# State attention and a gated causal convolution on one core: one PSUM pool of eight banks for three, and a new table of issue

## The chip, the core and the metric

The kernel runs on one core of a Trainium2 chip. Its engines run side by side, each through its own list of instructions in order: PE (TensorE: matmuls and transposes; PEld is its weight load), DVE (VectorE), ACT (ScalarE), POOL (GpSimd), and SP (SyncE), which here does nothing but issue the DMAs. An instruction waits for the data that it reads and for the buffer that it writes. PE writes to PSUM, a memory of eight banks of 128 partitions x 512 fp32 words; ACT and DVE read it there. All other tiles lie in SBUF.

The metric is the time of one execution in microseconds (us), as the median of several runs. One execution was recorded by the profiler; its rows are what this document reads.

## The reference

All inputs are fp32: `x` (8 batches, 8 heads, 512 rows, 64), `state` (8, 8, 32, 64), and three weights: two of 512 x 512 and a convolution of 5 taps x 512 channels (their values come as 64-bit floats and are decoded on the chip).

```python
scale = 1 / sqrt(D)
a     = softmax(scale * x @ state.T)          # (B,H,512,32)
xread = a @ state                             # (B,H,512,64)
a2    = softmax(scale * state @ x.T)          # (B,H,32,512)
sread = a2 @ x                                # (B,H,32,64)
u = concat([xread, sread], axis=2)            # heads side by side: (B,544,512)
gate_pre = sum over k in 0..4 of conv_w[k] * u shifted down by 4-k rows
y = (sigmoid(gate_pre) * (u @ w_val)) @ w_out # (B,544,512)
```

## The kernel before

**Tiles and steps.** Channels lie on the partitions: 512 channels are four blocks of 128, which are four pairs of heads. The program builds a list `steps` of small closures (one transpose, one softmax part, one tap, one projection tile) and then issues them in the order of a table of numbers, `ORDER` (L31 and on; the loop at L706 does it). A letter behind a number chooses the engine of a step that several can do: `a` ACT, `v` DVE, `g` POOL. Nothing else sets the order: each engine executes its instructions as the table lists them. The waits between engines come from the tiles. A tile name that has n buffers gives its n+1st tile the buffer of the first, and that tile's writer waits until all readers of the old one are done.

**The start.** SP loads the weights, the state and the first batch. `warm_up` (L243) multiplies the identity with itself, two matmuls to a step, four rows in the trace; nothing reads its result. The weights are decoded from their 64-bit words with elementwise steps: `words_scale`, `words_low` (L216), `words_clamp` (L221), `words_join` (L226) and `words_sign` (L231); those of `w_out` are then split into a high and a low part, `woh` and `wol`. `group_T` (L276, tile `sgp`) transposes the state of four batches.

**One batch.** Four `x_T` transposes (L309, `xTp`), copied to `xT`; the scores of state against x (L315; L337 for batches 0 to 2, tile `sc`), which serve both softmaxes. For the 512-row side: a transpose on DVE (L388, `sl`), the maximum `max_n` (L394), `sub_n` (L175, `sl<-sl,mx`), the exponential `exp_n` on ACT, the sums `sum_n` (L404 to L406), `scale_n` (L175, `ex<-ex,rc`), and `probs` (L412), a DVE transpose back. `high` and `low` split the result in two parts, `ah` and `al` (`combine` at L175 is the line of every two-operand elementwise step). For the 32-row side: `max_s` (L345), `exp_s`, transposes `exp_T` (L355, `e2p`), `state_read` (L365, `srp`), which also gives the tail its rows. `state_val` (L287, `sgv`) multiplies the state with `w_val`, and is split into `swh` and `swl`.

Then `read` (L421) writes the four tiles `xr` to PSUM. Per block of channels the convolution runs over `xr`: `gate_first` on ACT (L456), three `gate_tap` on DVE (L461), and the last tap as two steps, `gate_last` (L170 on ACT, L172 on DVE) and `gate_add` (L175, `acc<-acc,last`); `gate` on ACT makes the sigmoid by a tanh. Batch 0 is an exception: `read_conv` (L436) folds the taps into the matmul. `values` (L484) is six matmuls of 512 columns, `gated` (L487, `g`) multiplies gate and values, and `gh` (L162, L164, L166) and `gl` (L175) split the product for `project` (L492 to L494): twelve matmuls of 512 columns into one bank, then a copy to `o` and a store.

**The tail.** The 32 state rows of all batches go last, together: `tail_taps` (L518, `tacc`), `tail_values` (L544, `tval`), `tail_gated` (L548, `tg`) and two `tail_project` (`top`). Some projections of the last two batches stand between them.

**PSUM.** Three pools hold the eight banks: `tp` has two (`xTp`, `e2p`, `srp`, `srT`, `cwp`, `halo`), `sc` four (`sgp`, `sgv`, `sc`, `xr`) and `mm` two (`cwbp`, `warm`, `val`, `op`, `tval`, `top`). A tile takes the next bank of its own pool in turn.

Of the kernel before, what the change touches and what calls it, by code (L numbers as in the profile page):

```python
# [30 lines left out]
ORDER = """  # L31
41 50 5 8 0 53 10 107 42v 29 23 43 12 2 44v 11v 6 35 45 18 47 1 30v 13v 32v 14 105 15 915 916 917 918 114 59 3 36v 46
37 38v 919 920 921 922 16 17 19 31 48 104 39 52a 115v 40 60a 25 24v 110 108 106 83 33 61a 56 187 111a 55a 109a 21 51a
185 112 113a 54a 116 188 49a 186 26v 34 27 28 85 120 22v 58a 84v 86g 117 57a 62 288 193 66a 287 20a 118 189 194a 121
190a 195 122 124 285 87 125v 67a 89 103 123 191 196a 192a 64a 88 63a 119 126 65 133 77 134a 201 203 127 204 286 139 91
131 197 140a 198 202 132a 128g 130 295 142g 296a 289 141a 135 582 199 290a 90a 92g 216 136 129 217a 293 200 78a 71 205
79 294a 206v 386 93 207 291 143 80v 156 94 292a 101a 81 150 153 99a 144 137 208 184 72a 73 388 297 82 157 301 138a 385
147 298 158a 222 302 148 223a 303 102g 304 209g 74g 299 300 387 224 145 146a 213 225a 159g 168 210 226 164 227 75 97a
211a 169 165 149a 243v 228 212g 230 166a 242 76 214 314 315a 160 268 170a 244 487 215a 229a 245 167g 151 152a 395 389
235 171g 396a 161 486 390a 246 483 95a 231 264 218 247g 237 248 393 232 98g 249 394a 421 162a 219 238 422a 265 239 391  # L40
256 233g 100v 384 316 236v 392a 234 284 317a 423 251 266a 163g 257 220 305 96g 250a 267g 258a 397 318 252 424a 425 253
178 306g 322 313 485 254g 179v 307 319 399 255 308 269 175 398 484 401 402 309g 260 270g 176a 172 403 400 221a 323v
240g 68 325a 241 310 324 413 326 494 259g 271g 311a 173v 312g 327 261 329a 328 586 181 404 330 495a 492 342 262a 356
177 331 332 263v 343a 344 333v 182a 414a 69 272 493a 345 335 405g 337 334 350a 415 357 346 273a 338 180 488 406 364
347g 70a 348 339 407 358a 278 489v 183 365 412 349 336a 360 351 366a 408g 279a 584 340g 368 341 520 352 353 523a 280
274 367v 361 409 281 521a 410a 416a 359g 522 524 362g 282v 354g 426 355 369 434 436 275 441 428a 4 685 427 276a 411g
443 490 437 438 429 363g 430 583 370g 320 435a 491a 174 459 439g 371g 440 431 444 460 445 442a 321v 585 461g 455 683
496 500 497 277 501 378 432g 593 503 448 446g 682 433 589 456 379a 590a 380 375 504v 154 505 462g 463 498 499 155a 447
619 594v 417 587 506 376a 450 588a 464 467 465a 451 452 449v 507g 591 418 622v 502 453g 684 620a 419 420a 457a 454 372
508 621 509a 623 525 458g 511 373v 547 468 381 526 9 533 512 466g 527a 592a 549 550 783 510g 514 551 548a 781 552g  # L50
515a 382a 528 529 530 513a 566 535 553 692 531g 536 469v 782 595 534a 470g 516 599 885g 532 377 541v 567 784 517 597
554 596 686 555 602 537 474 600 693a 283 540 690 687a 598 688 480 383 603g 691a 556a 689a 604 542 543 538g 475v 539
601 780 694 879a 481a 605 482 568g 791 7 699 544 695 613 558 476 696 792a 606g 700 614a 562 787 698 607 697 624 569g
610 559 788a 632 701 789 790a 634 545g 710 640a 560g 557g 546 477 702g 563 639 608a 646 785 609g 641 471 478a 786a
564a 711a 642 635 681 479 643 661 633v 636 648 649 644g 611 561g 518 793 565g 472a 645 662 374 663a 612a 637g 650 647v
794 657 625 473 703 651v 795 797 519a 664g 638 881a 658 615 627 579 796 580a 712 626a 704 652 718 719a 713a 616 798
705g 581 628 720 886g 570 721v 799 629 630g 573 659a 706 722 631 707v 571a 800 723 731 653 574a 617 708g 745 738 665
811 733 734 732a 654 660g 746a 735 576 801g 666 747 655a 736v 737 667a 748 749 740 577a 656g 668g 802 756 739a 757
750v 817 725a 803 804g 724 678 818a 741 726 820a 882g 727 679a 758a 675 669 821 728 751 575 812a 676a 742 578 618a 709
714 805 806a 743g 819 822 729v 730 670a 744 715 809 883g 760 810a 845v 813 807g 831v 752 759g 830 761 671 832 833 753  # L60
762a 763v 834 764 765 672 835g 572 844 846 716 766a 808 847 823 855 848 836 673a 767g 754v 755v 856 837 863 814 815
849g 825 850 826 717v 864 816a 777 677 774 880v 838a 900 887a 884g 778a 865a 779 839 840 841 857a 674 842v 775v 771
902 888v 768 858v 772a 824a 843 899 859 866v 827 901 769a 828g 904 903 860 889 851 829 861a 891 862g 852 853a 905 773
894 854v 680 906 890 892 870 776 893 871a 895 907g 896 873 872 874a 908v 897v 867 898g 912 868a 913a 909 770 869 914
875 910v 911 876 877a 878
""".split()


# [666 lines left out]
```

## Time and profile before

| what | value |
| --- | --- |
| median of 3 runs | 247.87 us (246.74 to 247.98) |
| the profiled execution | 247.3 us, of which the span 245.5 us |
| busy | PE 231.2 us, DVE 206.3, ACT 151.0, POOL 127.0 |
| share of PE in the chain that ended last | 62% |
| moved by DMA | 22.88 MB |

The span runs from the first instruction to the last on the chip; the profiled execution has 1.8 us beside it. In the rows below, L with a number is a line of the kernel, `out<-in` names the tiles, `xN` counts instructions, and what stands in square brackets at the end of a row of the timeline is the idle time ahead of it and the instruction that ended this idle time. In rows of groups, the busy time in us and the mean of one in ns stand behind the first bar, the idle time behind the second. In rows of windows come, after the stretch and its length, the busy time of PE, PEld, DVE, ACT and POOL, the granted clock of PE, the DMA share and GB/s.

### The profile page before, as it was taken

The page shows a single profiled execution, that of the slowest core. Times are in us where ns is not written, and L with a number is a line of the kernel's source. Part 1 is how long each engine was busy: PE and PEld are TensorE (multiplying, and loading weights), DVE is VectorE, ACT ScalarE, POOL GpSimd, SP SyncE. Part 2 cuts the span into 40 slices and gives each one's busy share as a digit, 9 for nine tenths or more (in the row PEclk, how much of TensorE's full clock was granted, in tenths as well). Part 3 has the DMA queues.
Part 4 walks back from the last instruction along what each step waited for, and adds up shares of the span by engine and source line. Part 5 has one row for each costly group of instructions (what it writes and reads, how often), then busy time and mean ns, then how long its engine had stood idle before and what let it go on. Part 6 is the DMA issues. An engine that isn't in the chain of part 4 may idle for free.

```text
span 245.5 us, 5051 instructions
## 1 busy us (share of the span) xinstructions
PE 231.2 (94%) x1955; PEld 167.7 (68%) x1955; DVE 206.3 (84%) x325; ACT 151.0 (62%) x321; POOL 127.0 (52%) x101
## 2 busy tenths in 40 slices
PE   7976999899999999999999999999999999978994
PEld 7953463366677884866787778666766768867882
DVE  3299999999898998899899898998997899987200
ACT  2056977788647875754787769785696475433110
POOL 3001146289959267793575689928758380131200
PEclk9999999999999999999999999999999999999999
DMA  6939987000320309213801021110110302300224
GB/s 194 312 105 341 340 190 169 7 3 0 88 78 10 85 24 277 62 28 88 225 34 53 3 96 62 69 43 3 43 44 3 132 0 85 128 0 3 85 76 138
DMA packets 34549, 22.88 MB, mean 93 GB/s; under 512 B 26058, under 2 KB 29150, under 8 KB 34526
## 3 DMA queue, kind: packets, MB, share of 16 engines
q1 hardware_dynamic: 34526, 22.57, 30.2%
q8 instruction: 15, 0.25, 0.4%
q14 instruction: 8, 0.07, 0.1%
HBM read 13.65 MB, written 8.91 MB: 92 GB/s over the span
## 4 chain that ended last, share of the span: by engine, by line
PE 62%; DVE 24%; DMA 5%; issue 4%; ACT 2%; SPq 1%; DVEq 0%; ACTq 0%
PE val L484 12%; PE op L492 11%; PE op L494 10%; PE op L493 10%; DMA vw<-w_val 4%; PE xTp L309 3%; DVE acc L461 3%; PE xr L421 3%; DVE tacc L518 3%; PE srp L365 3%; DVE g L487 2%; PE e2p L355 2%; PE sgv L287 2%; PE sc L315 2%; DMA ow<-w_out 2%
## 5 line engine op out<-in xcount | busy, mean ns | idle before, releaser
L461 DVE SCALAR_TENSOR_TENSOR acc<-xr,cw,acc 128x509 f32<-128x509 f32 (+2 forms) x84 | 60.6, 739 | 3.8 <-ACT xt L457 2.7
L492 PE MATMUL op<-woh,gh 128*128 128x512 f32 x128 | 52.1, 407 | 1.5 <-DVE g L487 1.1
L494 PE MATMUL op<-woh,gl 128*128 128x512 f32 x128 | 50.4, 394 | 0.0
L493 PE MATMUL op<-wol,gh 128*128 128x512 f32 x128 | 50.1, 392 | 0.0
L175 POOL TENSOR_TENSOR acc<-acc,last 128x508 f32<-128x508 f32 x22 | 28.6, 1304 | 27.6 <-DVE acc L461 22.5
L175 POOL TENSOR_TENSOR gl<-g,gh 128x512 fp32r<-128x512 f32 x25 | 33.0, 1326 | 9.0 <-ACT gh L162 8.4
L492 PEld LDWEIGHTS op<-woh,gh 128*128 128x128 f32 x128 | 24.0, 188 | 13.5 <-DVE g L487 4.0
L162 ACT COPY o<-op 128x512 f32<-128x512 f32 x26 | 15.3, 590 | 21.6 <-PE op L494 21.6
L175 POOL TENSOR_TENSOR ex<-ex,rc 128x1024 f32<-128x1024 f32 x8 | 15.4, 1919 | 25.3 <-DVE rc L406 23.5
L494 PEld LDWEIGHTS op<-woh,gl 128*128 128x128 f32 x128 | 24.0, 188 | 5.4
L493 PEld LDWEIGHTS op<-wol,gh 128*128 128x128 f32 x128 | 24.1, 188 | 4.6
L484 PE MATMUL val<-ah,swh 128*128 128x512 f32 x56 | 24.1, 430 | 1.1 <-DVE g L487 1.1
L473 ACT ACTIVATE sig<-acc 128x512 f32<-128x512 f32 x28 | 17.8, 637 | 9.1 <-POOL acc L175 6.2
L487 DVE SCALAR_TENSOR_TENSOR g<-sig,val 128x512 f32<-128x512 f32 x32 | 21.5, 674 | 2.2 <-PE val L484 1.0
L309 PE MATMUL xTp<-ident,x 128*128 128x128 f32 x128 | 19.2, 279 | 3.7 <-DMA x<-x 2.2
L162 ACT COPY xT<-xTp 128x512 f32<-128x512 f32 x29 | 17.1, 594 | 9.0 <-PE xTp L309 8.8
L484 PE MATMUL val<-ah,swl 128*128 128x512 f32 x56 | 22.1, 395 | 0.0
L484 PE MATMUL val<-al,swh 128*128 128x512 f32 x56 | 22.1, 394 | 0.0
L456 ACT ACTIVATE acc<-xr,cw 128x512 f32<-128x512 f32 x28 | 19.3, 699 | 4.3 <-PE xr L421 3.9
L162 ACT CAST gh<-g 128x512 fp32r<-128x512 f32 x24 | 15.1, 633 | 9.8 <-DVE g L487 9.8
L309 PEld LDWEIGHTS xTp<-ident,x 128*128 128x128 f32 x128 | 14.3, 140 | 9.9 <-issue 1.9
L175 POOL TENSOR_TENSOR al<-sl,ah 128x1024 fp32r<-128x1024 f32 x7 | 17.1, 2443 | 4.5 <-ACT xt L162 3.6
(132 smaller groups left out, 456.3 us busy)
## 6 DMA issues: line engine op xcount, KB each, us to landing
x<-x SPq DMA_DIRECT2D x32, 256.0 KB
out<-o SPq DMA_DIRECT2D x32, 256.0 KB
vw<-w_val SPq DMA_DIRECT2D x4, 512.0 KB
ow<-w_out SPq DMA_DIRECT2D x4, 512.0 KB
sg<-state SPq DMA_DIRECT2D x8, 64.0 KB
z<-state SPq DMA_DIRECT2D x16, 32.0 KB
out<-to SPq DMA_DIRECT2D x8, 64.0 KB
cww<-conv_w SPq DMA_DIRECT2D x1, 20.0 KB
```

The lines of the kernel that those rows point to most:

```text
L162: nc.scalar.copy(out, in_)
L175: (nc.vector if e == "DVE" else nc.gpsimd).tensor_tensor(out, a, b, op=how)
L309: nc.tensor.transpose(get("xTp", b, pr)[:, j * P:(j + 1) * P], t, ident)
L365: nc.tensor.matmul(get("srp", b)[NS * q:NS * q + NS, g * D:(g + 1) * D], get("e2T", b, g)[:, j, NS * q:NS * q + NS], heads[:, j, NG * q + ...
L456: nc.scalar.mul(get("acc", b, pr), pt, cw[:, HALO, pr:pr + 1])
L461: nc.vector.scalar_tensor_tensor(acc[:, d:], get("xr", b, pr)[:, :S - d], cw[:, HALO - d, pr:pr + 1], acc[:, d:], op0=ALU.mult, op1=ALU.add)
L473: nc.scalar.activation(get("sig", b, pr), get("acc", b, pr), AF.Tanh, scale=0.5)
L484: nc.tensor.matmul(get("val", b, k), w, a, start=(i == 0), stop=(i == len(parts) - 1))
L487: nc.vector.scalar_tensor_tensor(get("g", b, k), get("sig", b, k), 1.0, get("val", b, k), op0=ALU.add, op1=ALU.mult)
L492: nc.tensor.matmul(pt, gh, woh[:, k], start=(k == 0), stop=False)
L493: nc.tensor.matmul(pt, gh, wol[:, k], start=False, stop=False)
L494: nc.tensor.matmul(pt, gl, woh[:, k], start=False, stop=(k == NPR - 1))
```

## The change

It has two parts. All PSUM tiles come from one pool of eight banks: a tile takes the next bank in turn, whatever it holds. And the table `ORDER` is a new one: it lists all steps of the table before in another order, some with another letter, and 15 further warm-up steps.

```diff
-41 50 5 8 0 53 10 107 42v 29 23 43 12 2 44v 11v 6 35 45 18 47 1 30v 13v 32v 14 105 15 915 916 917 918 114 59 3 36v 46
...
+0 50 1 107 10 18 53 11a 65 41 42a 12 5 13g 14 43 23 7 35 44v 15 24a 45 36a 25 37 46 2 6 47 26v 29 915 916 917 918 919
+920 921 922 923 924 925 926 927 928 929 930 931 932 933 934 48 114 38v 106 19 104 64a 105 27 39 30a 55a 115a 20a 89
...
-        tp=(2, [P, 512], F32), sc=(4, [P, 512], F32), mm=(2, [P, 512], F32),
+        ps=(8, [P, 512], F32),
...
-        xTp=("tp", F32), e2p=("tp", F32), srp=("tp", F32), srT=("tp", F32), cwp=("tp", F32),
-        cwbp=("mm", F32), halo=("tp", F32), sgp=("sc", F32), sgv=("sc", F32), xr=("sc", F32), warm=("mm", F32), val=("mm", F32), op=("mm", F32), tval=("mm", F32), top=("mm", F32),
+        xTp=("ps", F32), e2p=("ps", F32), srp=("ps", F32), srT=("ps", F32), cwp=("ps", F32),
+        cwbp=("ps", F32), halo=("ps", F32), sgp=("ps", F32), sgv=("ps", F32), sc=("ps", F32), xr=("ps", F32), warm=("ps", F32), val=("ps", F32), op=("ps", F32), tval=("ps", F32), top=("ps", F32),
...
-            pool = ps if tag in ("tp", "sc", "mm") else work
+            pool = ps if tag == "ps" else work
```

Steps that change their engine, each with its new count: `sub_n` of batches 0 to 2 goes from DVE to POOL (all eight are there now) and `scale_n` of batch 1 from POOL to DVE; of `gh`, two go from DVE and two from POOL to ACT (28 on ACT, 4 on POOL); of `gl`, four more go to POOL (29 there, 3 on DVE); of `gate_last`, five from DVE to ACT (25 and 3); of `gate_add`, two from DVE to POOL (24 and 4). Of the decoding, eight steps `words_scale` or `words_clamp` leave DVE (seven to ACT, one to POOL) and one `words_clamp` comes from POOL to DVE; two parts of `long_T` come from ACT to DVE; some dozen copies and splits move, most of them from DVE to ACT.

Three places of the order are shown, of before and of the change apart. A row gives line, operation, `out<-in` and shape of an instruction; the last number in a tile's name only counts tiles.

PE at the start, before: ten warm-up steps, of which the last stands first here, then the first transpose of x (`xTp`), five more warm-ups, the convolution's transposes (`cwp`, `cwbp`) and the transpose of the state (`sgp`).

```order
L243 MATMUL warm_148<-ident 128x128 x2
L309 MATMUL xTp_3_151<-ident,x_98 128x128 x4
L243 MATMUL warm_158<-ident 128x128 x2
...
L243 MATMUL warm_176<-ident 128x128 x2
L247 MATMUL cwp<-ident,cwf 128x20
L259 MATMUL cwbp_182<-cwf,sel 128x128 x4
L276 MATMUL sgp_189<-ident,sg_123 128x128 x4
L309 MATMUL xTp_1_205<-ident,x_98 128x128 x4
L309 MATMUL xTp_0_210<-ident,x_98 128x128 x4
```

The same place now; the first two rows are the last two of 26 warm-up steps in a row.

```order
L243 MATMUL warm_201<-ident 128x128 x2
L243 MATMUL warm_204<-ident 128x128 x2
L276 MATMUL sgp_207<-ident,sg_139 128x128 x4
L309 MATMUL xTp_3_212<-ident,x_90 128x128 x4
L259 MATMUL cwbp_219<-cwf,sel 128x128 x4
L243 MATMUL warm_237<-ident 128x128 x2
L309 MATMUL xTp_2_240<-ident,x_90 128x128 x4
L243 MATMUL warm_246<-ident 128x128 x2
L247 MATMUL cwp<-ident,cwf 128x20
L309 MATMUL xTp_0_256<-ident,x_90 128x128 x4
```

The state's transpose stands behind 26 warm-up steps where 15 stood before, and ahead of all transposes of x.

DVE between the sums of batch 1's softmax and what follows, before (`ws` and `wc` are tiles of the decoding of `w_out`, the number behind `o_` its block).

```order
L226 SCALAR_TENSOR_TENSOR ws_o_1_483<-wc_o_1_477,ws_o_1_483 128x512
L404 TENSOR_REDUCE sm_1_560<-ex_1_491 128x32
L405 TENSOR_SCALAR sm_1_560<-sm_1_560 128x32
L406 RECIPROCAL rc_1_563<-sm_1_560 128x32
L216 TENSOR_SCALAR ws_o_0_569<-ow0_0_479 128x512
L231 SCALAR_TENSOR_TENSOR ws_o_1_483<-ow1_1_341,ws_o_1_483 128x512
L487 SCALAR_TENSOR_TENSOR g_0_0_582<-sig_0_0_556,val_0_0_543 128x512
```

The same place now.

```order
L404 TENSOR_REDUCE sm_1_639<-ex_1_632 128x32
L405 TENSOR_SCALAR sm_1_639<-sm_1_639 128x32
L406 RECIPROCAL rc_1_642<-sm_1_639 128x32
L221 TENSOR_SCALAR wc_o_2_620<-wc_o_2_620 128x512
L226 SCALAR_TENSOR_TENSOR ws_o_1_441<-wc_o_1_410,ws_o_1_441 128x512
L175 TENSOR_TENSOR ex_1_632<-ex_1_632,rc_1_642 128x1024
L216 TENSOR_SCALAR ws_o_2_652<-ow0_2_485 128x512
L231 SCALAR_TENSOR_TENSOR ws_o_1_441<-ow1_1_350,ws_o_1_441 128x512
L226 SCALAR_TENSOR_TENSOR ws_o_2_652<-wc_o_2_620,ws_o_2_652 128x512
L216 TENSOR_SCALAR ws_o_0_732<-ow0_0_412 128x512
L412 STREAM_TRANSPOSE sl_1_408<-ex_1_632 128x1024
```

`scale_n` of batch 1 (`ex_1<-ex_1,rc_1`) is now on this engine, and four steps of decoding stand between it and `probs(1)`; the first product `g_0` comes behind them.

DVE in the last part, before (`_7_0` is block 0 of batch 7).

```order
L461 SCALAR_TENSOR_TENSOR acc_7_0_2610<-xr_7_0_2474,cw_68,acc_7_0_2610 128x509
L518 SCALAR_TENSOR_TENSOR tacc_1_2687<-xt_73,cw_68,tacc_1_2687 128x256 x4
L487 SCALAR_TENSOR_TENSOR g_7_2_2779<-sig_7_2_2744,val_7_2_2747 128x512
L518 SCALAR_TENSOR_TENSOR tacc_0_2781<-xt_73,cw_68,tacc_0_2781 128x256 x4
L487 SCALAR_TENSOR_TENSOR g_7_0_2800<-sig_7_0_2790,val_7_0_2783 128x512
L175 TENSOR_TENSOR gl_7_0_2830<-g_7_0_2800,gh_7_0_2802 128x512
L548 SCALAR_TENSOR_TENSOR tg_1_2833<-tsig_1_2777,tval_1_2764 128x512
```

The same place now.

```order
L175 TENSOR_TENSOR acc_7_0_2697<-acc_7_0_2697,last_7_0_2770 128x508
L487 SCALAR_TENSOR_TENSOR g_7_2_2794<-sig_7_2_2749,val_7_2_2682 128x512
L518 SCALAR_TENSOR_TENSOR tacc_1_2743<-xt_73,cw_68,tacc_1_2743 128x256 x4
L487 SCALAR_TENSOR_TENSOR g_7_3_2803<-sig_7_3_2787,val_7_3_2704 128x512
L487 SCALAR_TENSOR_TENSOR g_7_0_2845<-sig_7_0_2828,val_7_0_2654 128x512
L548 SCALAR_TENSOR_TENSOR tg_1_2867<-tsig_1_2811,tval_1_2755 128x512
L518 SCALAR_TENSOR_TENSOR tacc_0_2843<-xt_73,cw_68,tacc_0_2843 128x256 x8
```

All products `g` of batch 7 now come ahead of `tg_1`, and the eight taps `tacc_0` stand behind `tg_1`, where four of them stood between `g_7_2` and `g_7_0`. On PE, the four `values` of batch 7 now stand ahead of the four projections of batch 6; before, two of them stood behind those, one of the two behind the first of the `tail_values`.

More of the change, by code (lines that the diff above doesn't have):

```diff
@@ L31 @@
 ORDER = """
-41 50 5 8 0 53 10 107 42v 29 23 43 12 2 44v 11v 6 35 45 18 47 1 30v 13v 32v 14 105 15 915 916 917 918 114 59 3 36v 46
[L33 to L65, printed above, removed]
+0 50 1 107 10 18 53 11a 65 41 42a 12 5 13g 14 43 23 7 35 44v 15 24a 45 36a 25 37 46 2 6 47 26v 29 915 916 917 918 919
@@ new lines @@
+920 921 922 923 924 925 926 927 928 929 930 931 932 933 934 48 114 38v 106 19 104 64a 105 27 39 30a 55a 115a 20a 89
+935 112 28 4 113a 52a 31 16 108 185 54a 188 21 110 32v 109a 111a 33 936 120 51a 17 186 116 40 90a 34 189 91 195 49a
+22a 122 62 56 191 123 92g 133 187 60v 193 286 118 77 119 287 121 59 285 190a 117 131 58a 288 57a 130 124 139 192a 196a
+194a 93 134a 63a 125g 61a 141a 197 198 78a 71 66v 201 132a 184 291 199 94 293 79 103 8 126 292a 135 83 294a 127 68 385
+295 296a 202 289 290a 200 388 128g 67a 101a 203 937 297 205 136 142g 129 80v 301 214 145 303 386 204 140a 143 302 299
@@ new lines @@
+387 146a 215a 84a 298 206g 486 213 151 207 216 208 304 86v 144 81 209v 85 69 70a 152a 168 137 150 217a 148 72a 82 222
+153 147 154 487 155a 87 218 225a 73 284 156 74g 149a 219 210 138a 300 484 169 316 97a 75 88 227 76 211a 317a 228 160
+170a 157 230 158a 226 223a 212g 485 95a 224 229a 159v 98g 164 231 165 314 250a 249 171g 235 256 220 583 315a 232 221a
+389 391 390a 395 251 237 233g 166a 392a 252 396a 161 167g 393 394a 318 253 234 313 421 319 422a 397 238 96g 236a 264
+257 402 384 423 254g 162a 99a 268 403 398 399 255 260 163g 401 239 400 269 258a 270a 305 100g 424a 102g 242 240v 322
@@ new lines @@
+306g 325a 243a 307 413 323a 414a 259g 425 181 326 241 172 244 494 245 182a 320 173a 246 308 309g 324 404 321a 415 261
+492 483 493a 247g 495a 488 175 262a 310 263g 327 586 176v 311a 342 312v 343a 178 248 416a 328 405g 335 344 368 265
+271g 585 345 346 266a 179a 406 347g 489a 330 356 348 350a 490 337 364 331 174 332 365 267g 329a 349 360 407 338 333g
+275 272 682 491a 351 334 276a 339 352 357 520 183 408g 353 409 685 336a 273a 358a 340g 354g 523a 359g 410a 341 274 426
+521v 524 281 582 366a 412 177 361 427 428a 584 411g 278 367g 429 522 362a 355 430 434 436 282a 683 496 431 369 363g
@@ new lines @@
+437 417 780 497 459 432g 279a 370a 448 435a 498 418 499 500 371g 449a 503 450 455 280 438 451 504g 587 433 456 439g
+452 441 378 591 505 440 457a 506 283 507g 453g 501 460 372 588a 373a 684 443 502 508 375 379v 592a 442a 277 525 454
+461g 376a 444 445 512 467 526 528 529 589 458g 446g 513a 468 514 593 533 463 509a 515a 447 530 784 462g 781 511 180
+535 527a 381 547 548a 536 590a 419 549 594a 595 537 382a 420a 550 377 464 619 469g 531g 551 510g 465g 532 599 782 534a
+692 540 600 470g 596 622a 686 687a 566 601 693a 597 552g 688 620a 598 602 603g 562 553 621 613 690 623 541a 689a 567
@@ new lines @@
+554 691a 542 516 466g 604 694 783 517 543 605 699 700 606g 374 544 545g 696 614a 695 607 568a 480 555 481a 697 546
+569g 471 482 472a 473 624 608a 791 785 698 538v 610 380 563 639 641 642 643 556a 557g 474 786a 625 9 558 518 539 475a
+789 632 701 640a 633v 627 609g 519a 564a 611 634 628 612a 790a 644g 645 681 477 626a 661 635 559 646 636 653 702g 703
+478a 560a 648 787 629 565g 712 637g 479 792a 788a 561g 662 649 718 713a 793 881a 719a 615 704 663a 650 797 795 630g
+638 616 794 879a 647a 885a 664g 886v 631 573 710 705g 654 798 570 721a 720 651g 800 617 574a 801g 706 711a 722 796
@@ new lines @@
+571a 799 809 655a 707a 709 657 618a 723 731 732a 808 714 715 658 733 725a 724 652 579 659a 476 580a 581 726 734 708g
+727 716 656g 665 660g 735 810a 811 736g 883a 717a 764 802 745 812a 728 729g 747 666 576 748 667a 730 577a 813 738 803
+740 749 817 752 383 818a 668g 741 804g 814 756 746v 672 753 750g 737 742 805 754a 739a 751 757 760 673a 822 819 758a
+674 755g 743g 820v 765 821 806a 575 759v 675 678 766a 744 844 572 846 830 832 815 807g 761 847 669 679a 833 831a 767g
+816v 848 851 834 762a 855 837 880g 884g 845a 835v 763g 839 859 849g 882g 836 676a 677 840 823 841 825 838v 863 887a
@@ L66 @@
+826 888v 777 771 827 899 900 842g 856 843 901 904 857a 824a 772a 774 850 680 858v 828v 773 860 670a 671 902 864 865a
+861g 862g 903 894 866g 829 768 889 852 905 778a 853a 890 769a 779 906 895 854g 891 873 892 907a 870 908v 893 578 896
+874a 897a 898v 867 871a 872 875 770 912 775v 913a 914 868v 869 909 876 776 910a 911 877a 3 878
 """.split()
```

## The prediction

> **What bounds the kernel now.** I read the page first: busy times, slices, the chain of waits.
>
> ```profile
> span 245.5 us, 5051 instructions
> PE 231.2 (94%) x1955; PEld 167.7 (68%) x1955; DVE 206.3 (84%) x325; ACT 151.0 (62%) x321; POOL 127.0 (52%) x101
> PE   7976999899999999999999999999999999978994
> DVE  3299999999898998899899898998997899987200
> PE 62%; DVE 24%; DMA 5%; issue 4%; ACT 2%; SPq 1%; DVEq 0%; ACTq 0%
> ```
>
> PE is full in nearly all slices from the eighth on; DVE is full from the third on, but PE holds 62% of the chain. So the span has to be split. The windows below (stretch, its length, then busy PE, PEld, DVE, ACT, POOL) cut it where `read(1)` begins, at 47.89, and where PE ends.
>
> ```profile
> 0.00:47.89 47.89, 41.00 (x428) 27.02 (x429) 38.63 (x72) 28.10 (x63) 12.60 (x22) 1.00 0.72 213
> 47.89:241.90 194.01, 190.23 (x1527) 140.68 (x1527) 167.69 (x254) 122.31 (x258) 114.42 (x79) 1.00 0.21 64
> 12.30:47.60 35.30, 30.51 (x363) 16.62 (x361) 34.62 (x60) 26.57 (x61) 10.71 (x10) 1.00 0.69 200
> 196.00:242.00 46.00, 42.83 (x206) 34.94 (x205) 30.48 (x48) 16.50 (x34) 10.88 (x8) 1.00 0.17 62
> ```
>
> From 47.89 on PE idles 194.0 - 190.2 = 3.8 us, and 3.2 of it lies in the tail (last row: 46.0 - 42.8). From 12.3 to 47.6 it is DVE that is never idle (34.6 of 35.3). A busy PE can still be badly fed; the timeline says it is not:
>
> ```profile
> 76.96 0.50 PE L492 MATMUL op<-woh,gh 128*128 128x512 f32 x1
> 77.30 0.40 PE L493 MATMUL op<-wol,gh 128*128 128x512 f32 x1
> 77.53 0.39 PE L494 MATMUL op<-woh,gl 128*128 128x512 f32 x1
> ```
>
> Matmuls of 512 columns start every 0.23 us, though one shows 0.39 to 0.50. The first of them, right behind a `read`, takes 0.34 to the next: 0.11 more where PE changes from fp32 to fp32r operands. So there are three stretches: a start that DVE sets, 148 us that PE's work sets, and a tail with PE's waits:
>
> ```profile
> 94.35 0.51 PE L492 MATMUL op<-woh,gh 128*128 128x512 f32 x1 [0.52 <-DVE g L487]
> 202.40 0.50 PE L492 MATMUL op<-woh,gh 128*128 128x512 f32 x1 [0.61 <-DVE g L487]
> 217.36 0.51 PE L484 MATMUL val<-ah,swh 128*128 128x512 f32 x1 [0.88 <-DVE g L487]
> 221.63 0.39 PE L544 MATMUL tval<-xth,wvh 128*128 128x256 f32 x1 [1.17 <-DVE g L487]
> 223.70 0.47 PE L492 MATMUL op<-woh,gh 128*128 128x512 f32 x1 [0.38 <-DVE tg L548]
> ```
>
> These five sum to 3.56 us, nearly all idle time of the long stretch. All wait for DVE.
>
> **The start, term by term.** Its rows:
>
> ```profile
> 1.81 7.50 PE L243 MATMUL warm<-ident 128*128 128x128 f32 x40 [1.81 <-POOL ident masks.py:199]
> 9.59 2.40 PE L243 MATMUL warm<-ident 128*128 128x128 f32 x20
> 13.20 0.63 PE L276 MATMUL sgp<-ident,sg 128*128 128x128 f32 x4
> 17.28 2.67 PE L337 MATMUL sc<-xT,sTl 128*32 128x256 f32 x32
> 30.66 1.10 PE L365 MATMUL srp<-x,e2T 128*32 128x64 f32 x64 [0.26 <-ACT xT L162]
> 33.70 4.61 PE L436 MATMUL xr<-a,z 32*64 32x512 f32 x80
> 38.24 1.98 PE L484 MATMUL val<-a,sw 128*128 128x512 f32 x4
> 42.13 1.09 PE L287 MATMUL sgv<-wv,sT 64*32 64x512 f32 x16
> 47.89 1.47 PE L421 MATMUL xr<-sl,z 32*64 32x512 f32 x16 [0.82 <-DVE sl L412]
> 49.29 1.23 PE L355 MATMUL e2p<-ident,e 128*128 128x128 f32 x8
> ```
>
> A warm-up step is four rows. Ahead of `sgp` now stand 26 steps, 104 rows: the first 40 as before (until 9.3), the other 64 at 2.40/20 = 0.12, 7.7 us. So `sgp` starts at 17.0, not 13.2. Its data are no reason to wait: it ran at 13.2 with them, and on SP one load of 512 KB fewer stands ahead of the state's (block 1 of `w_val` has gone behind; its reader `sgv` came 13 us later). Before, the first scores came 4.08 us behind `sgp`, 17.28. The same piece now holds four x transposes, two spreads and three more warm-ups, about 3.6 to 4 us of PE work; I take 3.9: scores at 20.9, 3.6 late. From scores to `read_conv` I keep the old 16.4 us (DVE chain): 37.3. From there PE has `read_conv` 4.6, two `values(0)` of 1.8 each (38.24 to the next step at 40.06; a row's length runs over its successor's start), one `sgv` 1.0, one `srp` 1.05, two `e2p` 1.07, `sgp`, `srT` and small ones 1.1: 12.4, so **`read(1)` at 49.7**, 1.8 later. But by the order PE has then done `srp(1)`, `sgp(1)`, two more `e2p` and two small reads, less one `values(0)`: 1.05 + 0.5 + 1.07 + 0.1 - 1.8 = 0.9 more of work that was due behind `read(1)` before. **Net +0.9.**
>
> **The long stretch.** PE's real work is the same. Of three warm-up steps between real work two are gone and one remains (the fourth now stands behind the last matmul and hides under the copy and store of the last tile); the chain prices one:
>
> ```profile
> 101.41 0.45 PE warm L243 x4
> ```
>
> **-0.9.** Counted on PE's order from `read(1)` on, changes between fp32 and fp32r fall from 71 to 56. Half of 15 are in the direction that costs 0.11: **-0.8**; bounds 0 and 15 x 0.11 = -1.6.
>
> What moves between DVE, ACT and POOL is priced by the groups:
>
> ```profile
> L175 POOL TENSOR_TENSOR sl<-sl,mx 128x1024 f32<-128x1024 f32 x5 | 9.6, 1920 | 2.6 <-DVE mx L394 2.6
> L175 DVE TENSOR_TENSOR sl<-sl,mx 128x1024 f32<-128x1024 f32 x3 | 4.1, 1357 | 0.0
> L175 DVE TENSOR_TENSOR gl<-g,gh 128x512 fp32r<-128x512 f32 x7 | 5.7, 829 | 0.8 <-ACT gh L162 0.7
> L175 POOL TENSOR_TENSOR gl<-g,gh 128x512 fp32r<-128x512 f32 x25 | 33.0, 1326 | 9.0 <-ACT gh L162 8.4 <-PE sc L315 0.5
> L175 POOL TENSOR_TENSOR acc<-acc,last 128x508 f32<-128x508 f32 x22 | 28.6, 1304 | 27.6 <-DVE acc L461 22.5 <-ACT last L170 3.1 <-DVE last L172 1.3
> ```
>
> Three `sub_n` take 4.1 off DVE, four `gl` 3.3; with the other letters, each step at the mean of its group, DVE loses about 19 us of its 206, ACT gains 17.5 (to 169), POOL 3 (130). In the long stretch that is worth nothing by itself: PE has 190.2 of 194 there, so a cheaper DVE can at most take the 3.8 of idle time. If the cover went, each `gl` on POOL would add 1.33 - 0.83 = 0.5 to the path of its projection. One bank's ring of eight instead of 2+4+2 lets PE run ahead further with transposes and products but makes the next tile wait for the oldest of any kind; a bank here waits mostly for ACT or DVE to copy, and no quoted wait was for a bank. I set it at 0; it can gain no more than the idle time already counted, and as its other bound I take a wait like the shortest above, 0.38, once in each of eight batches: +3.0.
>
> **The tail.** PE's last waits were for `g` of batch 7, whose DVE work had the tail's taps between. Now `values(7)` come ahead of the last projections. Between `read(7)` and `project(7,2)`, PE has 7 projections and 4 values, 108 matmuls at 0.23 = 24.8, and four `tail_values` of 12 at half that, 5.5: 30 us. DVE's work until the last `g` of batch 7 is about 19 to 20:
>
> ```profile
> L487 DVE SCALAR_TENSOR_TENSOR g<-sig,val 128x512 f32<-128x512 f32 x32 | 21.5, 674 | 2.2 <-PE val L484 1.0 <-ACT sig L473 0.8 <-POOL gl L175 0.3
> L518 DVE SCALAR_TENSOR_TENSOR tacc<-xt,cw,tacc 128x256 f32<-128x256 f32 x16 | 10.4, 651 | 0.9 <-ACT tacc L512 0.5
> L461 DVE SCALAR_TENSOR_TENSOR acc<-xr,cw,acc 128x509 f32<-128x509 f32 x28 | 20.7, 742 | 0.6 <-ACT last L170 0.2
> ```
>
> (12 taps 8.9, four `g` 2.7, eight tail taps 5.2, and some 3 us of copies and splits). So 10 us are spare, and the waits of the tail go; the eight `tacc_0` that now come last have 36 matmuls, 8.3 us, of three projections for their 5.2. I take 3.0 of the 3.6 (**-3.0**), since a new order leaves some waits of its own; bounds 0 and -3.8.
>
> **Sum.** 247.3 + 0.9 - 0.9 - 0.8 - 3.0 = 243.5 on the scale of the profiled execution. The median of the runs lies 0.57 above that: **244.1**. Its own range: 241 to 246.6.
>
> **POOL against DVE.** One row of the start warns of what a sum of durations leaves out:
>
> ```profile
> 40.17 1.92 POOL L175 TENSOR_TENSOR ex<-ex,rc 128x1024 f32<-128x1024 f32 x1 [0.57 <-DVE rc L406]
> 40.22 2.41 DVE L231 SCALAR_TENSOR_TENSOR ws_o<-ow,ws_o 128x512 int32<-128x512 int32 x1
> L231 DVE SCALAR_TENSOR_TENSOR wv<-vw,ws_v 128x512 int32<-128x512 int32 x4 | 2.7, 683 | 0.0
> 31.48 1.55 POOL L175 TENSOR_TENSOR z<-z,cwb 128x640 f32<-128x640 f32 x1
> ```
>
> The DVE step took 2.41 in place of 0.68 while POOL's ran: 1.73 lost. The new order takes this `ex` from POOL, but gives POOL three `sub_n` of the same width in the start. [...]
>
> **Rivals.** *B: the warm-ups hide and the start gets quicker.* Summed over DVE's new order with the old durations, its work from 12.3 to `probs(1)` is 28.8, not 35.3: two `sub_n` gone (2.7), scales and clamps on ACT, decoding of later blocks put behind; `scale_n(1)` is added. If the chain follows that sum, `read(1)` comes at 47.9 + 3.8 - 6.5 = 45.2, 4.5 before my forecast: 239.6. For it: DVE was full there. Against it: the chain also runs through PE, ACT and POOL, and the first 3.8 are lost ahead of it. Chance 0.12.
>
> *C: no change.* The 3.0 come back as waits for ACT or for banks, and the changes of operand type were hidden anyway (0.8): 244.1 + 3.8 = 247.9. For it: ACT is busy 122.3 of 194 in the long stretch, and most of its 17.5 more falls there, some 70% in all. Against it: all five waits named DVE. 0.12.
>
> *D: slower, by POOL in the start's chain.* Scores, maximum, `sub_n` on POOL, exponential, sums, `probs`: a serial chain, in which two `sub_n` cost 0.56 more each, two held DVE steps 1.73 each, and the `z` step (1.55) may stand ahead of `sub_n(1)` on POOL: 1.1 + 3.5 + 1.6 = 6.2 more, 250.3. It decides from the point where `read(1)` comes later than 53.5; then the other gains (4.7 less 0.9) are used up. For it: the start sets when all of PE's long stretch begins, and decoding steps with two inputs stand close by on DVE. Against it: DVE has other work meanwhile, and both held steps must fall on the chain. 0.13.
>
> *E: PE's clock falls between bursts.* All windows granted 1.00. A cold PE costs, by the first two rows of the start, 7.50 - 40 x 0.12 = 2.7 us each time; from two such times on the change is slower or equal, 249.5. It needs more idle time than the rows have, 0.4 to 1.2 at a time without a change of clock. [...] 0.04.
>
> **How the numbers follow.** Forecast 0.59, B 0.12, C 0.12, D 0.13, E 0.04. The likeliest is mine, 244.1. The range 239.5 to 249.5 takes in B, C and the nearer part of D, and leaves some 0.15 outside. A measurement can tell about 0.5%, 1.24 us, from no change: faster is below 246.6. Faster: 0.56 of mine, B, a little of C, 0.70; same: most of C, 0.03 of mine, 0.13; slower: D, E, 0.17.
>
> **What would show it.** `sgp` at 17 and `read(1)` near 49.7; one warm-up in the chain behind it; idle time of PE behind `read(1)` below 1.5 us, none before `project(7,2)`. B shows as `read(1)` at 45, D as `read(1)` behind 53 with `sl<-sl,mx` of POOL in the chain, C as idle rows that name ACT, E as a clock below 1.00 or first matmuls at 0.2 for 128 columns. I am wrong if PE's matmuls are not at 0.23 any more, or if `sgp` waits for anything but PE.

## The result: 2.5% faster, and PE almost without a wait

The changed kernel takes 241.85 us, the median of four runs (241.27 to 242.13), against 247.74 (246.74 to 247.98) before: a ratio of 0.9754, 95% interval 0.9725 to 0.9782. That is 5.9 us, where 3.8 (from 247.87 to 244.1) were forecast. The profiled execution took 241.91, its span 240.1, which is 5.4 less than before. The page:

```profile
span 240.1 us, 5167 instructions
PE 232.9 (97%) x2015; PEld 175.7 (73%) x2015; DVE 188.1 (78%) x296; ACT 165.0 (69%) x348; POOL 131.5 (55%) x103
PE   6999999989999999999999999999999999999994
PE 86%; DVE 5%; ACT 4%; POOL 3%; issue 2%; ACTq 0%; POOLq 0%; DVEq 0%
```

PE holds 86% of the chain where it held 62%. The busy times of DVE, ACT and POOL moved much as the prediction had summed them (187, 169, 130). The windows of the same kernel, cut at its `read(1)` (51.15), in the columns of before:

```profile
0.00:51.15 51.15, 48.12 (x572) 36.99 (x572) 35.74 (x66) 32.62 (x73) 11.71 (x21) 1.00 0.71 207
51.15:236.60 185.45, 184.49 (x1443) 138.60 (x1443) 152.35 (x231) 131.91 (x275) 119.74 (x82) 1.00 0.21 65
12.30:51.15 38.85, 37.63 (x503) 26.49 (x502) 30.48 (x54) 28.96 (x68) 9.54 (x8) 1.00 0.68 193
190.70:236.70 46.00, 46.00 (x227) 38.64 (x226) 29.62 (x45) 18.57 (x37) 14.97 (x12) 1.00 0.20 74
```

Three things are to be seen. The start got longer: `read(1)` is at 51.15, not 47.89. Behind it PE needs 185.5 us, not 194.0, and idles 0.96 of them, not 3.8; in the tail not at all. And in the start it is now PE that is full (37.6 of 38.85) and DVE that has time (30.5). The timeline of PE in the start:

```profile
1.81 14.39 PE L243 MATMUL warm<-ident 128*128 128x128 f32 x104 [1.81 <-POOL ident masks.py:199]
16.03 0.60 PE L276 MATMUL sgp<-ident,sg 128*128 128x128 f32 x4
21.81 2.23 PE L337 MATMUL sc<-xT,sTl 128*32 128x256 f32 x32
37.74 4.87 PE L436 MATMUL xr<-a,z 32*64 32x512 f32 x80
48.77 1.98 PE L484 MATMUL val<-a,sw 128*128 128x512 f32 x4 [0.63 <-DVE g L487]
51.15 1.11 PE L421 MATMUL xr<-sl,z 32*64 32x512 f32 x16
```

The 104 rows of warm-ups run until 16 us, and from there on PE goes from one step to the next.

Where the gain of PE's stretch behind `read(1)` came from, I took from the starts of its instructions: for each kind, the time from its starts to the next start, summed. From the first start to the last it is 193.6 us before and 185.5 now, 8.1 less. It contains the waits, which are counted with the step ahead of them.

| kind | before, us | after, us | what it is |
| --- | --- | --- | --- |
| `tval` | 8.73 | 5.68 | three waits of the tail, 3.05 |
| `srT` | 1.39 | 0.85 | the wait at 202 |
| `sgv` | 7.16 | 5.82 | the wait at 94, and gaps between steps |
| `e2p`, `srp`, `sgp`, `halo` | 13.62 | 10.66 | mostly steps that are now done ahead of `read(1)` |
| `values(0)` | 1.32 | 3.54 | one such step more behind it |
| `val`, `op` | 132.50 | 131.11 | waits and changes of operand type |
| `warm` | 1.34 | 0.70 | two steps fewer, one of them new behind the end |
| the rest (`sc`, `xr`, `xTp`, `top`) | 27.53 | 27.11 | |

Two things in the account of the change above were named wrongly. The three `sub_n` that go from DVE to POOL are those of batches 0, 1 and 4, so two of them lie in the start, not three (and of the decoding seven steps leave DVE, six of them to ACT). And a tile does not take the next bank strictly in turn. `sgp` is in one of the eight banks, and `cwbp` at 20.36 is the eighth PSUM tile behind it; taken in turn it would need the bank of `sgp`, which ACT still reads at 35.44:

```profile
20.36 0.48 PE L259 MATMUL cwbp<-cwf,sel 20*128 20x128 f32 x2
35.44 0.27 ACT L170 ACTIVATE sTl<-sgp 64x128 f32<-64x128 f32 x1
```

Counted along the table, from the first step that writes a tile to the last that reads it, the old order holds at most 2, 4 and 2 banks of its three pools at once, and the new one up to eight of the one pool.

### The profile page after: what moved, and what is told of

Its sections match the earlier page's. It is cut to its first block, busy times and chain, and to the rows that moved or that the text cites. A ratio compares the mean times of both kernels' runs of the same rounds, so it can differ in the third digit from the quotient of the medians.

```text
span 240.1 us, 5167 instructions
## 1 busy us (share of the span) xinstructions
PE 232.9 (97%) x2015; PEld 175.7 (73%) x2015; DVE 188.1 (78%) x296; ACT 165.0 (69%) x348; POOL 131.5 (55%) x103
## 4 chain that ended last, share of the span: by engine, by line
PE 86%; DVE 5%; ACT 4%; POOL 3%; issue 2%; ACTq 0%; POOLq 0%; DVEq 0%
PE val L484 17%; PE op L492 13%; PE op L494 12%; PE op L493 12%; PE warm L243 7%; PE xTp L309 5%; PE srp L365 3%; PE xr L421 3%; PE sgv L287 3%; PE tval L544 2%; PE e2p L355 2%; PE sc L315 2%; PE sc L337 2%; ACT xT L162 2%; POOL sl L175 1%
## 5 line engine op out<-in xcount | busy, mean ns | idle before, releaser
L461 DVE SCALAR_TENSOR_TENSOR acc<-xr,cw,acc 128x511 f32<-128x511 f32 (+2 forms) x84 | 59.7, 740 | 11.4 <-ACT xt L457 6.6
L175 POOL TENSOR_TENSOR gl<-g,gh 128x512 fp32r<-128x512 f32 x29 | 38.6, 1331 | 13.4 <-ACT gh L162 13.0
L175 POOL TENSOR_TENSOR acc<-acc,last 128x508 f32<-128x508 f32 x24 | 31.7, 1323 | 11.0 <-DVE acc L461 2.9
L162 ACT COPY o<-op 128x512 f32<-128x512 f32 x28 | 16.5, 590 | 20.2 <-PE op L494 14.8
L162 ACT CAST gh<-g 128x512 fp32r<-128x512 f32 x28 | 17.5, 629 | 7.6 <-DVE g L487 7.6
L243 PE MATMUL warm<-ident 128*128 128x128 f32 x132 | 18.8, 303 | 1.8 <-POOL ident masks.py:199 1.8
L175 POOL TENSOR_TENSOR sl<-sl,mx 128x1024 f32<-128x1024 f32 x8 | 16.3, 2034 | 7.6 <-DVE mx L394 7.6
L162 ACT COPY xT<-xTp 128x512 f32<-128x512 f32 x32 | 18.1, 599 | 3.0 <-PE xTp L309 2.9
L175 POOL TENSOR_TENSOR ex<-ex,rc 128x1024 f32<-128x1024 f32 x7 | 13.4, 1917 | 11.7 <-DVE rc L406 8.0
L243 PEld LDWEIGHTS warm<-ident 128*128 128x128 f32 x132 | 18.0, 218 | 2.1 <-POOL ident masks.py:199 1.8
```

What stands on the lines that cost most here:

```text
L162: nc.scalar.copy(out, in_)
L175: (nc.vector if e == "DVE" else nc.gpsimd).tensor_tensor(out, a, b, op=how)
L243: nc.tensor.matmul(get("warm", i)[:, j * P:(j + 1) * P], ident, ident, start=True, stop=True)
L461: nc.vector.scalar_tensor_tensor(acc[:, d:], get("xr", b, pr)[:, :S - d], cw[:, HALO - d, pr:pr + 1], acc[:, d:], op0=ALU.mult, op1=ALU.add)
```

## The experiments

Two theories stood against each other. The prediction's: the pool alone is worth nothing, the order of the tail takes PE's waits away, and the letters are hidden. Its rival, from the rows of before: the instructions that waited there are three `op`, a `val` and a `tval`, and none of these reads `g` or `tg`. What they write is a bank of `mm`, of which there were two, and `val` held one until `g` had read it. So these were waits for banks. And a question of its own: what do 26 warm-up steps cost? The kernel before was run again beside the others, and took 247.32, 246.61 or 246.54 us where it took 247.74 above; so where two runs with different such figures are compared, a difference of medians is uncertain by about 1 us, and the ratios are the better measure.

**The pool alone.** The table of before, with the one pool:

```diff
-        tp=(2, [P, 512], F32), sc=(4, [P, 512], F32), mm=(2, [P, 512], F32),
+        ps=(8, [P, 512], F32),
```

> The table of issue of before, with the one pool of eight banks. Theory P (banks): the waits of PE for `g` in the tail were waits for the two banks of `mm`, which `val` held until `g` had read it, since an `op` tile does not read `g` itself. Then the pool alone takes away most of the five waits of before (3.6 us idle, up to 5 with the drained pipe): 243 to 244.5 us, and no idle row of PE in the tail names DVE g. Theory O (order), the one of the prediction, which set the pool at 0: the waits stay, 247 to 248.5 us, and they go only with the new order of the tail.

Measured: 245.69 us against 247.32 before, ratio 0.9937 (0.9901 to 0.9973). The timeline of PE has two idle times left behind `read(1)`:

```profile
54.12 0.50 PE L484 MATMUL val<-ah,swh 128*128 128x512 f32 x1 [0.55 <-DVE g L487]
220.43 0.50 PE L492 MATMUL op<-woh,gh 128*128 128x512 f32 x1 [2.23 <-ACT gh L162]
```

None of the five waits of before is there (the one at 54.12 is another): with the old order, the pool took them away. Theory P is right on what they were. But the median is above its 243 to 244.5 (the two of its ten executions with a mean clock of 1.00 took 243.79 and 244.66), since a new, longer wait has come: 2.23 us for `gh`, which `op` does read. Two rows of DVE say why `gh` is late:

```profile
215.97 3.16 DVE L518 SCALAR_TENSOR_TENSOR tacc<-xt,cw,tacc 128x256 f32<-128x256 f32 x4 [0.50 <-ACT tacc L512]
219.05 0.68 DVE L487 SCALAR_TENSOR_TENSOR g<-sig,val 128x512 f32<-128x512 f32 x1
```

Four taps of the tail stand ahead of the last product. And the wait costs more than itself. Windows of the same kernel behind it:

```profile
220.00:222.00 2.00, 1.57 (x6) 1.01 (x7) 1.59 (x3) 0.79 (x2) 0.22 (x1) 1.00 0.00 0
222.00:224.60 2.60, 2.60 (x8) 2.08 (x7) 2.21 (x4) 0.25 (x1) 0.99 (x1) 0.53 0.00 0
```

The granted clock is 0.53 there, in a stretch that begins 1.8 us after PE has gone on, and its matmuls of 512 columns start every 0.43 us in place of 0.23.

**The pool and one edit of the tail.** The same kernel, with the last product ahead of those taps:

```diff
-889 851 829 861a 891 862g 852 853a 905 773 894 854v 680
+889 851 829 861a 852 853a 854v 891 862g 905 773 894 680
```

> The table of before with the one pool, and in the tail one edit: the last product of batch 7 (`gated`, its `gh` and `gl`, block 0) stands ahead of the four taps `tacc_0` on DVE instead of behind them. With the pool alone PE waited 2.23 us there for `gh` and its clock was 0.53 for the next 2.6 us. Theory T (this wait and what the clock did behind it are what the pool alone gave back): both go, 3.3 to 4 us less than with the pool alone: 241.7 to 242.6, level with the changed kernel. Theory M (the wait moves on to the products behind it, or to the tail's own): 244 to 245.5.

Measured: 243.29 us against 246.61, ratio 0.9864 (0.9804 to 0.9923); its profiled execution took 244.46. The wait of 2.23 is 0.32 now, and the clock of the tail is full:

```profile
221.30 0.50 PE L494 MATMUL op<-woh,gl 128*128 128x512 f32 x1 [0.32 <-DVE gl L175]
195.00:240.00 45.00, 43.74 (x214) 36.07 (x212) 30.93 (x50) 16.94 (x34) 10.92 (x8) 1.00 0.18 64
```

So theory T is right on the tail; the median is 0.7 above its bound. Part of what is missing lies in the start of the profiled execution, which the edit does not touch:

```profile
21.08 1.79 PE L309 MATMUL xTp<-ident,x 128*128 128x128 f32 x8 [2.32 <-DMA x<-x]
23.00:25.50 2.50, 1.95 (x10) 1.98 (x11) 2.50 (x4) 2.13 (x5) 0.00 (x0) 0.50 1.02 353
```

PE waited 2.32 us for x, and its clock was 0.50 behind. The one of its four executions with a mean clock of 1.00 took 242.15. By the ratios, the pool and three moved steps give 1.4%, where the whole change gives 2.5%; and the change pays for 11 more warm-up steps in that, without which it gives 3.9% (the run with fewer, below). So the new table does more than these three steps.

**Seven banks.** The changed kernel with one bank less:

```diff
-        ps=(8, [P, 512], F32),
+        ps=(7, [P, 512], F32),
```

> The changed kernel with seven banks in its pool in place of eight. Theory P (the number of banks that the next tile may choose from is what took the waits away): some waits of PE come back, 0.4 to 1.0 us each at a few places, together 1 to 4 us: 243 to 246. Theory O: banks are not short in the new order, within 0.7 us of the changed kernel.

Measured: 259.27 us against 247.32, ratio 1.0465 (1.0408 to 1.0522), 17 us more than with eight, far above what either theory gave. The timeline of PE has waits of this kind all along; four of them:

```profile
59.86 0.47 PE L484 MATMUL val<-ah,swh 128*128 128x512 f32 x1 [1.38 <-DVE g L487]
88.70 0.51 PE L492 MATMUL op<-woh,gh 128*128 128x512 f32 x1 [2.49 <-ACT e2T L162]
...
164.98 0.51 PE L492 MATMUL op<-woh,gh 128*128 128x512 f32 x1 [0.68 <-ACT e2T L162]
...
199.60 0.50 PE L484 MATMUL val<-ah,swh 128*128 128x512 f32 x1 [0.53 <-DVE last L172]
```

An `op` does not read `e2T`: where it waits for the copy of an `e2p`, it waits for a bank. So banks decide, and the new order is fitted to eight of them: in one pool a tile of any kind that is read late can stop PE (2.49 us for the copy of an `e2p`). The idle times of PE behind `read(1)` sum to 9.7 us here, where they are 1.0 with eight banks, and the granted clock is 0.94 from 90 to 110, behind the wait of 2.49; the rest of the 17 us was not taken apart. The new order cannot be had with the three pools of before. Followed along the tables, `read_conv` of batch 0 needs four banks of `sc` while one of the four still holds a score tile of batch 2, whose last readers stand behind steps that wait for `read_conv`; so it would stand still. What the order is worth without the pool is therefore not shown.

**Fewer warm-ups.** The changed kernel without 11 of the 26:

```diff
-... 915 916 917 918 919 920 921 922 923 924 925 926 927 928 929 930 931 932 933 934 48 114
+... 915 916 917 918 919 920 921 922 923 48 114
```

> The changed kernel without 11 of the 26 warm-up steps that stand in a row ahead of the state's transpose (steps 924 to 934), so 15 stay ahead of it as before. Theory W (they cost): `sgp` starts near 11.5 to 13 in place of 16.0, and since PE is never idle behind it, `read(1)` and the end come 2 to 3.5 us earlier: 238.5 to 240. Theory H (they hide): the first x, the decoding on DVE or the softmax's chain sets the start, PE waits there instead, `read(1)` stays within 0.7 us of 51.15 and the time near 241.5.

Measured: 237.69 us against 247.32, ratio 0.9612 (0.9581 to 0.9644).

```profile
1.81 9.67 PE L243 MATMUL warm<-ident 128*128 128x128 f32 x60 [1.81 <-POOL ident masks.py:199]
11.31 0.60 PE L276 MATMUL sgp<-ident,sg 128*128 128x128 f32 x4
46.43 1.11 PE L421 MATMUL xr<-sl,z 32*64 32x512 f32 x16
```

`sgp` and `read(1)` both come 4.72 us earlier, and the span is 4.7 shorter (by the medians it is 4.2, by the ratios 3.5). The 11 steps, 44 rows at 0.108, were paid to the full: theory W, and more than it gave. Without them the new order has a start that is 1.5 us shorter than that of before.

**Still fewer.** 18 of the 26 taken out, so 8 stay:

> The changed kernel with 8 warm-up steps ahead of the state's transpose (18 of the 26 taken out), the other five kept. Theory W: `sgp` can start when the state has landed, 9.5 to 10.5, so `read(1)` at 45 to 45.8 and 236.4 to 237.2. Theory C (the warm-ups are what gets PE to its full clock): the transposes behind them take 0.2 us each for a longer time, `read(1)` is at 46.4 or later and the time 237.7 or more. Theory H: PE waits for data in the start and nothing is gained, 237.3 to 238.

Measured: 241.1 us against 246.61, ratio 0.9803 (0.9725 to 0.9881): 3.4 us more than with 15 (4.7 by the ratios). The wait and two windows behind it:

```profile
11.96 0.81 PE L276 MATMUL sgp<-ident,sg 128*128 128x128 f32 x4 [4.59 <-DMA sg<-state]
12.00:16.00 4.00, 4.00 (x18) 3.45 (x19) 3.72 (x8) 2.14 (x5) 0.00 (x0) 0.53 0.89 294
16.00:20.00 4.00, 4.00 (x20) 3.44 (x20) 1.26 (x3) 1.84 (x5) 0.00 (x0) 0.61 0.78 266
```

PE ran out of warm-ups before the state had landed, idled for 4.59 us, and had a clock of 0.53 and 0.61 for the next 8. That is theory C, in another form: here the warm-ups bridged the time until the data were there, and behind the gap the clock was lower (a mean of 0.972 to 0.986 in the four executions, where the four of the run with 15 have 1.00).

**No cover in the start.** 15 ahead of `sgp`, and the five warm-up steps between the steps of batches 0 to 2 taken out:

> The changed kernel with 15 warm-up steps ahead of the state's transpose, as in the run with fewer, and without the five that stand between the steps of batches 0 to 2 at the start. Theory W (PE's work still sets the start): five times 0.54 us, `read(1)` at 43.7 in place of 46.4, and 235 us. Theory H (now the chain over POOL, ACT and DVE ends last): PE shows idle rows in the start, `read(1)` at 45.5 to 46.5 and 236.8 to 237.8. If an idle time above 2 us arises, the clock may fall behind it and the time be 238 or more.

Measured: 236.95 us against 246.61, ratio 0.9604 (0.9554 to 0.9654); against the run with these five (0.9612) no difference that the intervals show. `read(1)` is at 46.01, only 0.42 earlier, and PE waits where the warm-ups had been:

```profile
29.22 1.93 PE L337 MATMUL sc<-xT,sTl 128*32 128x256 f32 x32 [0.78 <-ACT xT L162]
32.45 0.28 PE L444 MATMUL halo<-a,z 32*64 32x4 f32 x4 [0.62 <-DVE a L412]
43.63 1.98 PE L484 MATMUL val<-a,sw 128*128 128x512 f32 x4 [0.95 <-DVE g L487]
```

Theory H: with 15 steps the chain over the other engines and PE's own work end almost together.

**`sub_n` of batches 0 and 1 back on DVE**, in the changed kernel:

```diff
-125g ... 206g
+125v ... 206v
```

> The changed kernel with `sub_n` of batches 0 and 1 back on DVE. Theory PE (PE's work, warm-ups among it, sets the start; POOL's longer `sub_n` is hidden): `read(1)` within 0.6 us of 51.15 and the time within 0.7 us of 241.85. Theory D (POOL's part in the softmax chain costs time): `read(1)` 1 to 3 us earlier, 239 to 241.

Measured: 244.85 us against 246.61, ratio 0.9908 (0.9871 to 0.9945), 3 us slower than the changed kernel (3.8 by the ratios). Both theories fell: POOL's longer `sub_n` is not the price, it spares one. `sub_n(1)` here, the same step of the changed kernel, a wait of PE here and a window behind it:

```profile
39.99 1.18 DVE L175 TENSOR_TENSOR sl<-sl,mx 128x1024 f32<-128x1024 f32 x1
37.64 2.09 POOL L175 TENSOR_TENSOR sl<-sl,mx 128x1024 f32<-128x1024 f32 x1
50.27 3.55 PE L484 MATMUL val<-a,sw 128*128 128x512 f32 x4 [2.18 <-DVE g L487]
52.00:54.00 2.00, 2.00 (x6) 0.86 (x4) 0.16 (x2) 0.00 (x0) 2.00 (x1) 0.51 1.05 238
```

On DVE the step stands behind others in the queue: it ends at 41.17, where POOL's longer one ends at 39.73, and the softmax behind it and the first product of batch 0 are 1.5 us later. So PE waits 2.18 us in place of 0.63, and the clock behind it is 0.51 from 52 to 54. Of the ten executions, the two with a mean clock of 0.999 took 242.68 each, the eight with 0.991 to 0.993 took 244.31 to 245.77: some 2 us of the loss go with the clock, which hardly fell in those two.

**The old letters behind `read(1)`.** The changed kernel, with the 66 steps behind `read(1)` that changed their engine put back on their old one, for instance:

```diff
-326 241 172 244 494 245 182a
+326 241 172 244 494 245 182v
```

> The changed kernel with the 66 steps behind `read(1)` that have changed their engine put back on the engine that they had before, in the new places. Theory hidden (the prediction's: behind `read(1)` PE sets the time, and what moves between DVE, ACT and POOL is worth nothing by itself): PE's stretch behind `read(1)` within 1 us of 185.5, 241.2 to 243. Theory fed (PE needs these letters): rows of idle time of PE that name DVE, 3 us or more in sum, and a fall of the clock where one is above 2 us: 244 to 248.

Measured: 249.68 us against 246.54, ratio 1.0116 (1.0057 to 1.0175), 7.8 us slower than the changed kernel (9 by the ratios) and slower than before. Busy times, two idle rows of PE and a window:

```profile
PE 235.7 (95%) x2015; PEld 175.6 (71%) x2015; DVE 203.3 (82%) x318; ACT 154.3 (62%) x327; POOL 129.0 (52%) x102
100.10 1.12 PE L421 MATMUL xr<-sl,z 32*64 32x512 f32 x16 [1.96 <-ACT swh L170]
117.87 0.51 PE L492 MATMUL op<-woh,gh 128*128 128x512 f32 x1 [1.10 <-DVE g L487]
90.00:130.00 40.00, 36.62 (x269) 25.81 (x268) 37.82 (x55) 25.98 (x53) 24.50 (x19) 1.00 0.37 103
```

DVE is busy 37.8 of 40 us there, and PE stands still for 3.4 of them. This shows that the letters carry the new order; it does not show that they were needed with the old one, whose order was another.

**More changes of operand type.** Nine fp32 steps of the changed kernel moved between two fp32r steps, as here `x_T(4,3)` (494) between two projections (181 and 172):

```diff
-425 181 326 241 172 244 494 245 182a
+425 181 494 326 241 172 244 245 182a
```

> The changed kernel with nine fp32 steps of PE (five x transposes, four state_val) moved ahead to stand between two fp32r steps: 74 changes between fp32 and fp32r behind read(1) in place of 56, the same work. Theory S: a change costs about 0.1 us in either direction, +1.8 us: 243.3 to 244. Theory half (the prediction's): 0.05 a change, +0.9: 242.5 to 243. Theory none: the changes are hidden by the weight loads, within 0.4 us of the changed kernel.

Measured: 246.11 us against 247.32, ratio 0.9951 (0.993 to 0.9973), 4.3 us above the changed kernel, more than any of the three theories. The trace says that it measured something else:

```profile
66.66 0.47 PE L484 MATMUL val<-ah,swh 128*128 128x512 f32 x1 [0.73 <-DVE sl L388]
71.50 0.50 PE L492 MATMUL op<-woh,gh 128*128 128x512 f32 x1 [0.93 <-DVE swl L295]
100.67 0.50 PE L492 MATMUL op<-woh,gh 128*128 128x512 f32 x1 [0.64 <-DVE swl L295]
```

Tiles written earlier hold banks for longer, and PE waits for these. The price of a change of type stays open; `val` and `op`, where it falls, gained 1.4 us between before and after, waits included.

**The best version.** The changed kernel with 15 warm-up steps ahead of `sgp` and none between real work:

> The changed kernel with 15 warm-up steps ahead of the state's transpose and no other between real work (the five of the start and the one behind `read(1)` taken out). Against the run without the five: one warm-up step of 0.45 us less in the stretch that PE sets, 236.2 to 236.8. If that step covered a wait, no change: 236.8 to 237.3.

Measured: 236.35 us (235.5 to 237.34) against 246.54, ratio 0.9581 (0.9539 to 0.9624): `read(1)` at 45.38. That is faster than both kernels, 1.8% below the changed one by the ratios, but not clearly below the two runs from which it comes.

**The state's loads earlier**, in this best version, ahead of two loads of weights:

> The kernel of the run e10_best with the four loads of the state (64 KB each) two loads of 512 KB earlier on SP. In the run without cover PE waited 0.39 us for the state; 0.78 and 0.69 for `xT`. Theory L (these loads are late): `sgp` 0.3 to 0.5 us earlier, and the chain from there too: 235.8 to 236.4. Theory X (the weights' decoding and the x loads, now later, set the chain): no gain or up to 1.5 us longer.

Measured: 237.37 us against 246.54, ratio 0.962 (0.9573 to 0.9667). Not faster, and by the intervals not clearly slower; the x that comes behind is late instead, theory X:

```profile
13.60 0.63 PE L309 MATMUL xTp<-ident,x 128*128 128x128 f32 x4 [0.62 <-DMA x<-x]
17.70 2.42 PE L337 MATMUL sc<-xT,sTl 128*32 128x256 f32 x32 [1.72 <-ACT xT L162]
```

## Why the prediction was right or wrong, step by step

**The direction and the range were right, the sum too small by 2.3 us, and one of its steps was wrong in kind.** That it came so near is luck in part, since errors of both signs met: the start cost 1.6 us more than was summed, PE's stretch behind `read(1)` gained 2.7 more (7.4 without the moved steps, where 4.7 were forecast), and another 0.5 came behind PE's last matmul.

*The start: right in mechanism, too small.* `sgp` came at 16.03 (17.0 was said; the rows took 0.108 each behind the first 40, not 0.12), scores at 21.81 (20.9), `read(1)` at 51.15 (49.7). The term that was mis-sized most is the piece from `sgp` to the scores, 5.77 us where 3.9 were taken. The net was +2.5 (3.26 later, less the 0.74 that the moved steps make in the table) in place of +0.9. That the last 11 of these warm-ups are paid in full is shown by the run without them: 4.72. Rival B was right on DVE, which had time, but its condition, that the warm-ups hide, did not hold; with 15 of them the start was indeed shorter than before.

*"I set it at 0 ... no quoted wait was for a bank": wrong.* This step failed. The five quoted waits were of three `op`, a `val` and a `tval`, for `g` or `tg`, which none of them reads; the releaser of a wait is not always what the instruction reads, it can be the reader of what it overwrites. The pool with the old order took all five away, and one bank less cost 17 us.

*The tail, -3.0: right in its result, with half of the reason.* No wait is left there. But the order alone was not what did it: the pool took away the waits for banks, and the order the one for `gh` (2.23 us, and the clock behind it) that came to light then. The pool alone gives 1.6 us; the order cannot be run without the pool.

*"That is worth nothing by itself": wrong for this order.* Put back, the letters behind `read(1)` cost 7.8 us, and two `sub_n` in the start 3. The argument was that PE had only 3.8 us to gain; it overlooked what there was to lose. With one pool of banks, a late copy or product of any engine can stop PE (1.96 us for `swh` of ACT, 1.10 for `g` of DVE in that run), and DVE, busy 95% of a stretch, is late.

*Warm-ups behind `read(1)`, -0.9:* measured -0.64, since a piece of the one behind the last matmul is counted. *Changes of type, -0.8:* not settled. Idle time behind `read(1)` fell by 2.8 in the windows; the account by starts gives, without moved steps and warm-ups, 8.1 - 0.7 - 0.6 = 6.8, where the prediction had 3.8. So these waits cost more than the idle time their rows show (three rows of the tail sum to 2.43, the account to 3.05; the "up to 5 with the drained pipe" that was expected of the pool was an estimate that no run shows), and the rest, of which changes of type are a part, wasn't taken apart.

*Rival C* did not happen: one wait of 0.35 for ACT is left. *Rival D:* `z` and `sub_n(1)` stood in the chain on POOL, as it said, and yet the `sub_n` on POOL were worth 3 us. The two held DVE steps that it priced did not come either: beside the two `sub_n` no DVE step lost more than 0.10 us (`wc_o`, 0.52 in place of 0.42), and it was the `sub_n` that took longer, 2.29 and 2.09 us where POOL's took 1.92 before. A DVE step with one input was longer beside POOL as well: at 46.15 `ws_o<-ow` took 0.83 in place of 0.42, beside a `wc_o` of POOL.

*Rival E* did not happen: in the changed kernel all windows shown have a clock of 1.00, and the mean of the profiled execution is 0.998. But a lower clock behind a wait of PE, which is what it priced, was met in five of the experiments (the table under the last heading). Its 2.7 us each time was an estimate from the first two rows of the start; in the run with `sub_n` on DVE some 2 us go with the clock.

## What to carry to other kernels

Ask of every wait whether the instruction reads what released it; if not, it waits for a buffer, and more buffers or one shared pool can remove it where no reordering is needed. A full engine's small idle total says what relief can gain, not what the same steps cost if they come late. And filler work ahead of the first real step was paid in full here once the data were there (4.72 us for 11 steps), but a gap in its place (4.59 us) was paid again in the clock behind it (0.53 and 0.61 for 8 us).
